# Transposing the attention probabilities by DMA in a DiT adaLN attention block

## The chip, the cores and the metric

The kernel runs on one core of one Trainium2 chip. The metric is the device time of one execution in microseconds (us), lower is better. Durations inside an execution come from one profiled execution of the kernel, and times in the trace count from the start of its span.

## The reference

Everything is bf16, with B = 2 batches, N = 256 tokens each and D = 1152 channels. A conditioning vector gives shift, scale and gate; the attention has one head of width D.

```python
mod = (_silu(c) @ w_mod).reshape(B, 6, 1, D)
shift_a, scale_a, gate_a, shift_m, scale_m, gate_m = [mod[:, i] for i in range(6)]
h = _layernorm(x, axis=-1) * (1 + scale_a) + shift_a
qkv = h @ wqkv
q, k, v = (qkv[..., :D].copy(), qkv[..., D:2 * D].copy(), qkv[..., 2 * D:].copy())
p = _softmax(jnp.einsum('bqd,bkd->bqk', q, k) * D ** (-0.5), axis=-1)
a = jnp.einsum('bqk,bkd->bqd', p, v) @ wo
return x + gate_a * a
```

`p` is a 256 x 256 matrix for each batch, and it is this matrix that is transposed.

## The kernel before

The 512 tokens are four tiles of 128 (`TT = 4`, two for each batch, `NQ = 2`), and the 1152 channels are nine blocks of 128 (`KT = 9`). All matmuls contract over the 128 partitions.

The work goes through these stages on TensorE: a first stage in which x is normalized and transposed while the weights arrive, and K is accumulated; Q, in nine blocks of 128 channels (`ps`, 512 columns wide); the scores `s_ps` (36 matmuls, 18 for each batch); V, in twelve groups; the transposes of P; P times V; the output projection with the gate and the residual.

For V, `v_group(gidx)` (line 577) computes one of 4 token tiles times one of 3 chunks of 384 channels: nine matmuls into a PSUM buffer `ps`, and one eviction into `v_sb` by ScalarE, or by VectorE for the eighth and later groups with an even index. The pool `psum` has six buffers, and `psum_a` and `psum_b` have one each.

While TensorE computes V, the softmax runs on VectorE and ScalarE. `row_max(b)` scales the scores and takes the row maximum, `exps(b)` takes the exponentials with their row sums, and `normalized(b)` (line 567) multiplies by the reciprocal of the row sum and writes P in bf16 to `pns[b]`, one instruction for each of two tiles of 128 query rows. In the trace the tile is called `pn`. Between these VectorE runs `gate_step`, which accumulates the gate into `gacc`; after the last step GpSimd sums `gacc` over the partitions into `gate_bc`, once for each batch (line 603).

P times V needs P with the key index on the partitions. So line 612 takes a PSUM tile `pT_ps` for each batch, line 615 has TensorE transpose the four 128 x 128 blocks of `pns[b]` into it, and line 617 copies it to `pT` in SBUF, on VectorE for batch 0 and on ScalarE for batch 1:

```python
    for gidx in range(TT * NCH - 1):
        v_group(gidx)
...
    v_group(TT * NCH - 1)
```

Eleven value groups run ahead of the transposes (the first two lines) and the twelfth behind them (the last), so that the copies to `pT` run while TensorE does the twelfth group.

P times V (36 matmuls, 18 for each batch, batch 0 first) multiplies `v_sb` as weights with `pT` into `ps`, and VectorE and ScalarE in turn evict it to `attnT`. The output projection takes four token tiles of 3 chunks (the last tile has 5 smaller ones), nine matmuls each; VectorE multiplies by `gate_bc` (to `ga`) and adds x (to `o_sb`), and stores go out from the load queue, except for the very last piece, which ScalarE's queue stores.

The order on every engine is written out by hand. A recorder class wraps each engine (`vec`, `sca`, `ten`, `spq`, `gps` for VectorE, ScalarE, TensorE, the load queue on SyncE, and GpSimd), and `pin` at the end fixes that each engine executes its instructions in the order of the program. Therefore line 74, which stands inside the recorder, is the line of nearly every instruction in the profile, and instructions are told apart by the tiles that they write and read. The framework adds the semaphore waits that the data needs. The load queue `spq` issues all loads of x and the weights, the last of them three of `wo`, and then five of the six stores of the output.

Of the kernel before, what the change touches and what calls it, by code (L numbers as in the profile page):

```python
# [11 lines left out]
BF16 = mybir.dt.bfloat16  # L12
# [4 lines left out]
def kernel(  # L17
# [10 lines left out]
    P = 128  # L28
    B, N, D = x.shape
    T = B * N  # L30
    KT = D // P
    TT = T // P
    NQ = N // P
    CW = 384
    NCH = D // CW
# [20 lines left out]
    work = ctx.enter_context(tc.tile_pool(name="work", bufs=2))  # L56
    psum = ctx.enter_context(tc.tile_pool(name="psum", bufs=6, space=PSUM))
    psum_a = ctx.enter_context(tc.tile_pool(name="psum_a", bufs=1, space=PSUM))
    psum_b = ctx.enter_context(tc.tile_pool(name="psum_b", bufs=1, space=PSUM))
# [23 lines left out]
    ten = _Rec(nc.tensor, pe_seq)  # L83
    spq = _Rec(nc.sync, sp_seq)
# [11 lines left out]
    def tok(b):  # L96
        return slice(b * N, (b + 1) * N)

    ident = const.tile([P, P], BF16)
    gps.memset(ident, 0.0)  # L100
    gps.affine_select(
        out=ident, in_=ident, compare_op=ALU.not_equal, fill=1.0, base=0,
# [14 lines left out]
        out=pick, in_=pick, compare_op=ALU.is_ge, fill=0.0, base=0,  # L117
# [3 lines left out]
        out=pick, in_=pick, compare_op=ALU.is_ge, fill=0.0, base=NT - 1,  # L121
# [228 lines left out]
    def evac(idx, out_ap, in_ap):  # L350
        if idx % 2 == 0:
            return vec.tensor_copy(out=out_ap, in_=in_ap)
        return sca.copy(out=out_ap, in_=in_ap)
# [107 lines left out]
    for i in range(NEARLY):  # L461
        pool, tag = (psum_b, "pb") if i == 0 else (psum, "mm")
# [85 lines left out]
    nmxs, p_fs, rsums, pns = {}, {}, {}, {}  # L548
# [28 lines left out]
    def v_group(gidx):  # L577
        t, vc = divmod(gidx, NCH)
        wt = chunks_w[NCH + vc]
        ps = psum.tile([P, CW], F32, tag="mm")  # L580
        for k in range(KT):
            ten.matmul(
                ps, lhsT=hT[:, k, t * P : (t + 1) * P], rhs=wt[:, k, :],
                start=(k == 0), stop=(k == KT - 1),
            )
        evac(1 if gidx < N_V_EARLY else gidx, v_sb[:, t, vc * CW : (vc + 1) * CW], ps)
# [16 lines left out]
        ar = gps.partition_all_reduce(gate_bc[:, b, :], gacc[:, b, :], P, bass.bass_isa.ReduceOp.add)  # L603
        tc.add_manual_dep(ar.ins, gate_done, SYNC_SCHED, reason="keep gpsimd off the shared port")

    for gidx in range(TT * NCH - 1):
        v_group(gidx)

    attnT = act.tile([P, KT, T], BF16, tag="a2")
    pT_sbs = []  # L610
    for b in range(B):
        pT_ps = (psum_a if b == 0 else psum_b).tile([P, NQ, N], BF16, tag="pa" if b == 0 else "pb", name="pT_ps")
        for i in range(NQ):
            for j in range(NQ):
                ten.transpose(pT_ps[:, j, i * P : (i + 1) * P], pns[b][:, i, j * P : (j + 1) * P], ident)
        pT = work.tile([P, NQ, N], BF16, tag="pT")
        evac(b, pT, pT_ps)
        pT_sbs.append(pT)
    v_group(TT * NCH - 1)
    LASTW = 64  # L620
    TAILW = CW // 2
    wo_last = const.tile([P, KT, TAILW], BF16)
# [22 lines left out]
    for t in range(TT):  # L645
        b = t // NQ
# [68 lines left out]
```

## Time and profile before

| What | Value |
|---|---|
| Time, median of 3 runs | 99.29 us (99.03 to 99.8) |
| The profiled execution | 99.14 us |
| Its span, first to last instruction | 97.4 us |
| Granted TensorE clock | 1.000 |
| TensorE busy | 91.6 us (94%) |
| VectorE busy | 71.6 us (74%) |
| ScalarE busy | 34.4 us (35%) |
| GpSimd busy | 22.0 us (23%) |
| Eight transposes of P on TensorE | 70.52 us, 0.61 us from first start to last end |
| Two copies to `pT` | 415 ns (VectorE), 586 ns (ScalarE) |
| Traffic of the DMA engines | 21.06 MB, 216 GB/s in the mean |

PE stands for matmuls on TensorE and PEld for its weight loads, which overlap with them; DVE is VectorE, ACT is ScalarE, POOL is GpSimd and SP is SyncE. In the chain of work that ended last, each piece has its start, its length and the tile that it writes; x8 is a count of instructions. A group in the timeline has its start, the time from its first start to its last end, and in brackets the idle time before it with what ended it. Matmuls are pipelined, so the duration given for one of them overlaps with that of the next, and the sum of such durations is more than the time that they take.

### The profile page before, as it was taken

What the parts mean: (1) busy time and instruction counts of PE and PEld (TensorE: products, weight loads), DVE (VectorE), ACT (ScalarE), POOL (GpSimd) and SP (SyncE); (2) the same over time, 40 slices, a digit from 0 to 9 for tenths busy, and PEclk for the clock granted to TensorE, in tenths of its full rate; (3) what the DMA queues carried; (4) which work ended last, traced back from release to release, by engine and by line L of the source; (5) the groups of instructions that cost most, each with busy time, mean ns of one, the idle gap of its engine ahead of it and who ended that gap; (6) DMA issues with size and microseconds to landing.
All of it is one profiled execution on the core that took longest, in us unless ns stands there. A gap on an engine that the chain in (4) does not pass through costs nothing.

```text
span 97.4 us, 1833 instructions
## 1 busy us (share of the span) xinstructions
PE 91.6 (94%) x734; PEld 56.2 (58%) x739; DVE 71.6 (74%) x139; ACT 34.4 (35%) x69; POOL 22.0 (23%) x26
## 2 busy tenths in 40 slices
PE   3998989999999999999999999999999999999960
PEld 1347879554566444444458766666678766666660
DVE  1488667419985999999973999991039587999870
ACT  5098964220570962432240455231145400000010
POOL 6600006500000000000000000009999960062000
PEclk9999999999999999999999999999999999999999
DMA  2999999999999999999999100000000000303222
GB/s 59 311 351 396 359 399 364 400 403 405 390 384 393 392 411 377 373 373 371 401 414 372 55 0 0 0 0 0 0 0 7 0 0 0 121 0 121 100 72 77
DMA packets 17720, 21.06 MB, mean 216 GB/s; under 512 B 1712, under 2 KB 12208, under 8 KB 17712
## 3 DMA queue, kind: packets, MB, share of 16 engines
q1 hardware_dynamic: 17296, 20.89, 59.1%
q8 instruction: 6, 0.10, 0.4%
q10 hardware_dynamic: 416, 0.05, 0.3%
q14 instruction: 2, 0.02, 0.0%
HBM read 19.76 MB, written 1.18 MB: 215 GB/s over the span
## 4 chain that ended last, share of the span: by engine, by line
PE 91%; DVE 4%; issue 1%
PE ps L74 61%; PE acc L74 11%; PE junk_ps L74 6%; PE s_ps L74 4%; PE tp L74 2%; PE psH L74 2%; PE psE L74 1%; DVE o_sb L74 1%; DVE ga L74 1%; PE psL L74 1%; DVE hTs L74 1%; PE psM L74 1%; PE psSA L74 1%; DVE junk_rhs L74 1%; DVE stats L74 0%
## 5 line engine op out<-in xcount | busy, mean ns | idle before, releaser
L74 POOL PARTITION_ALL_REDUCE gate_bc<-gacc x2 | 13.7, 6887 | 47.0 <-DVE gacc L74 47.0
L74 DVE SCALAR_TENSOR_TENSOR gacc<-wG,scT_f,gacc 128x1152 f32<-128x1152 bf16 x16 | 22.7, 1418 | 0.5
L74 PE MATMUL ps<-wqv,hT 128*128 128x384 bf16 x108 | 17.9, 326 | 0.0
L74 PE MATMUL ps<-hT,wqv 128*128 128x512 bf16 x80 | 17.6, 379 | 0.1
L74 PE MATMUL ps<-wO,attnT 128*128 128x384 bf16 (+1 forms) x108 | 17.0, 319 | 0.0
L74 PEld LDWEIGHTS <-attnT 128*128 128x128 bf16 x126 | 11.3, 98 | 6.4
L74 PEld LDWEIGHTS <-hT 128*128 128x128 bf16 x108 | 10.5, 98 | 6.7
L74 PE MATMUL acc<-hTs,wK 128*128 128x128 bf16 (+2 forms) x88 | 13.4, 292 | 0.5 <-DVE hTs L74 0.3
L74 PEld LDWEIGHTS <-wK 128*128 128x128 bf16 x123 | 10.2, 97 | 6.4 <-issue 0.7
L74 PEld LDWEIGHTS <-wqv 128*128 128x128 bf16 x81 | 7.9, 98 | 9.6 <-DVE hT L74 0.4
L74 ACT CAST qkT<-ps 128x512 bf16<-128x512 f32 x10 | 5.8, 584 | 10.9 <-PE ps L74 10.9
L74 DVE TENSOR_TENSOR ga<-ps,gate_bc 128x384 f32<-128x384 f32 (+1 forms) x12 | 6.4, 537 | 2.4 <-PE ps L74 2.3
L74 ACT CAST v_sb<-ps 128x384 bf16<-128x384 f32 x10 | 4.7, 476 | 8.3 <-PE ps L74 8.2
L74 DVE TENSOR_TENSOR o_sb<-ga,x_sb 128x384 bf16<-128x384 f32 (+1 forms) x12 | 6.9, 578 | 0.4
L74 PE MATMUL junk_ps<-junk_rhs 128*128 128x512 bf16 x14 | 5.7, 577 | 1.5 <-DVE junk_rhs L74 1.5
L74 ACT CAST o_sb<-ps 128x128 bf16<-128x128 f32 (+1 forms) x2 | 0.5, 240 | 17.0 <-PE ps L74 17.0
L74 DVE TENSOR_TENSOR xnT<-xnT,rstd_bc 128x512 bf16<-128x512 bf16 x9 | 5.5, 681 | 0.0
L74 PE MATMUL ps<-hTs,wK 128*128 128x512 bf16 x19 | 4.9, 378 | 0.1
L74 DVE CAST attnT<-ps 128x512 bf16<-128x512 f32 (+1 forms) x6 | 3.5, 603 | 1.8 <-PE ps L74 1.8
L74 DVE BATCH_NORM_STATS2 stats<-x_sb 128x6 f32<-128x384 bf16 x6 | 3.2, 553 | 2.2 <-DMA x_sb<-in_x_dram 2.2
L74 ACT CAST qkT<-acc 128x512 bf16<-128x512 f32 x6 | 3.0, 611 | 4.1 <-PE acc L74 4.1
L74 DVE CAST v_sb<-ps 128x384 bf16<-128x384 f32 x2 | 1.1, 558 | 4.6 <-PE ps L74 4.6
(87 smaller groups left out, 94.7 us busy)
## 6 DMA issues: line engine op xcount, KB each, us to landing
wqv<-in_wqkv_dram SPq DMA_DIRECT2D x5, 864.0 KB, 10.0
wG<-in_w_mod_dram SPq DMA_DIRECT2D x3, 864.0 KB, 9.5
wO<-in_wo_dram SPq DMA_DIRECT2D x3, 864.0 KB, 8.8
wH<-in_w_mod_dram SPq DMA_DIRECT2D x4, 576.0 KB, 7.3
wS<-in_w_mod_dram SPq DMA_DIRECT2D x6, 288.0 KB, 6.4
wK<-in_wqkv_dram SPq DMA_DIRECT2D x6, 288.0 KB, 7.1
x_sb<-in_x_dram SPq DMA_DIRECT2D x4, 288.0 KB, 3.7
wqv<-in_wqkv_dram SPq DMA_DIRECT2D x3, 288.0 KB, 8.4
```

Of the source, the lines that this page charges most:

```text
L74: r = fn(*a, **k)
```

## The change

The eight TensorE transposes, the PSUM tile `pT_ps` and the two copies are removed. In their place the load queue issues one DMA for each half of P of each batch, four in all, which reads 128 query rows by 256 keys from `pns[b]` in SBUF and writes them transposed into `pT` in SBUF, as two blocks of 128 keys by 128 queries. In the program these stand ahead of all twelve value groups, and the twelve groups follow each other without a break. In the load queue they come after the loads of `wo` and before the stores of the output. TensorE's first weight load of P times V waits for the two DMAs of batch 0.

```diff
-    for gidx in range(TT * NCH - 1):
-        v_group(gidx)
-
     attnT = act.tile([P, KT, T], BF16, tag="a2")
     pT_sbs = []
     for b in range(B):
-        pT_ps = (psum_a if b == 0 else psum_b).tile([P, NQ, N], BF16, tag="pa" if b == 0 else "pb", name="pT_ps")
+        pT = work.tile([P, NQ, N], BF16, tag="pT")
         for i in range(NQ):
-            for j in range(NQ):
-                ten.transpose(pT_ps[:, j, i * P : (i + 1) * P], pns[b][:, i, j * P : (j + 1) * P], ident)
-        pT = work.tile([P, NQ, N], BF16, tag="pT")
-        evac(b, pT, pT_ps)
+            spq.dma_start_transpose(out=pT[:, :, i * P : (i + 1) * P], in_=pns[b][:, i, :])
         pT_sbs.append(pT)
-    v_group(TT * NCH - 1)
+    for gidx in range(TT * NCH):
+        v_group(gidx)
```

## The prediction

> **What bounds the kernel now.** I began with the page's busy shares, because the change takes work off TensorE, VectorE and ScalarE and gives some to the DMA engines, and I wanted to know which of these can move the end.
>
> ```profile
> PE 91.6 (94%) x734; PEld 56.2 (58%) x739; DVE 71.6 (74%) x139; ACT 34.4 (35%) x69; POOL 22.0 (23%) x26
> PEclk9999999999999999999999999999999999999999
> DMA  2999999999999999999999100000000000303222
> ```
>
> TensorE is busy for 94% of the span at an undiminished clock. One slice of the rows is 97.4 / 40 = 2.435 us, so the loads are over by about 56 us and the DMA engines are all but empty from there to about 82 us. A share of busy time is an average, so next I read the chain that ended last, in order of time (start, length, what), around the transposes and at the end.
>
> ```profile
> 50.67 3.93 PE s_ps L74 x36
> 54.60 16.09 PE ps L74 x99
> 70.69 0.45 PE pT_ps L74 x8
> 71.13 21.49 PE ps L74 x144
> 92.63 0.02 issue
> 92.65 0.57 DVE ga L74
> ```
>
> From 50.67 to 92.63 us the chain never leaves TensorE: scores, eleven value groups (11 x 9 = 99 matmuls), the eight transposes into pT_ps, then 144 matmuls (9 of the twelfth value group, 36 of P times V, 99 of the output projection). No other engine has a piece between them, so TensorE time removed here moves what follows, until another wait comes up. The length to use is the chain's 0.45 us. The 219 ns of one transpose in its tile's rows overlaps its neighbours: 8 x 219 ns would be 1.75 us, while the timeline below has 0.61 us from the first start to the last end.
>
> The third view is the timeline of the same stretch, for when P is ready, when its transpose is used, and what the copies stand beside.
>
> ```profile
> 57.23 0.62 DVE L74 TENSOR_SCALAR pn<-p_f,rinv 128x256 bf16<-128x256 f32 x2
> 59.29 0.61 DVE L74 TENSOR_SCALAR pn<-p_f,rinv 128x256 bf16<-128x256 f32 x2
> 70.52 0.61 PE L74 MATMUL pT_ps<-ident,pn 128*128 128x128 bf16 x8
> 70.72 0.56 DVE L74 CAST v_sb<-ps 128x384 bf16<-128x384 f32 x1 [2.37 <-PE ps L74]
> 71.17 0.59 ACT L74 COPY pT<-pT_ps 128x512 bf16<-128x512 bf16 x1 [1.43 <-PE pT_ps L74]
> 71.20 0.41 DVE L74 COPY pT<-pT_ps 128x512 bf16<-128x512 bf16 x1
> 72.27 2.77 PEld L74 LDWEIGHTS <-v_sb 128*128 128x128 bf16 x25
> 72.43 2.78 PE L74 MATMUL ps<-pT,v_sb 128*128 128x256 bf16 x24
> ```
>
> P of batch 0 is written by 57.85 us and P of batch 1 by 59.90 us, but pT is not read before 72.27 us. The copies run under the twelfth value group, and their engines next wait for TensorE.
>
> **The change part by part.** The sum is made against the profiled execution: 99.14 us, with a span of 97.4 us and 1.74 us around it. That is 0.15 us under the median of 99.29 us.
>
> *Removed from TensorE:* eight transposes, 0.45 us on the path. As a check, VectorE's eviction of the eleventh value group starts at 70.72 us and ScalarE's of the twelfth at 72.63 us, 1.91 us apart, where evictions of neighbouring groups start 1.46 us apart (64.87, 66.33): the difference is again 0.45 us. Term: -0.45 us, bounded by 0 and by the -0.61 us of the timeline.
>
> *Removed from VectorE and ScalarE:* copies of 415 and 586 ns, off the path. After them VectorE is idle 1.46 us and ScalarE 0.88 us before their next work, each ended by TensorE. Term: 0.
>
> *Moved:* nothing but the twelfth value group, which now follows the eleventh directly. TensorE's later matmuls keep their order. The two spare PSUM buffers are not used by anything after, so that is worth 0.
>
> *Added to the load queue:* four DMA transposes, each 128 x 256 bf16 (64 KB), behind the three loads of wO, whose issue is over at 46.4 us, and ahead of the five output stores on this queue, the first of which is issued at 82.13 us. Each waits for its half of P on VectorE and for the DMA that used its completion semaphore before, a weight load long landed. Behind a waiting transpose stand only the other transposes and those stores, and the stores are not due until after pT has been used. In the trace no DMA of this sort occurs. Its nearest rows by size are the output stores, 1.7 us to landing for 48 KB and 2.1 us for 288 KB. The tiny load of c_sb, in 256 runs of 18 bytes, took 3.0 us. From below, four in flight together cannot be issued faster than the 0.36 us of a plain issue, so 57.6 + 2 x 0.36 + 1.7 = 60.0 us for batch 0, and some 62 us for batch 1. From above I let nothing overlap and let the hardware move single elements: 32768 per DMA over 16 engines at about 11 ns of engine time each (queue q10: 416 packets in 0.3% of 16 engines' span, 0.003 x 97.4 x 16 / 416) is 23 us, plus 1.7 us, or 24.7 us each. I take 2.1 us each, one after another, since the store is the row nearest in size and the engines are idle: the fourth lands at 57.6 + 4 x 2.1 = 66.0 us.
>
> *When this is due:* TensorE's weight load ahead of P times V now waits for the first two transposes, at 72.27 - 0.45 = 71.8 us; the other two are due half of the 36 matmuls later, at 73.8 us. With d for the time of one DMA, batch 0 needs 57.6 + 2d below 71.8 (d below 7.1 us) and batch 1 needs 57.6 + 4d below 73.8 (d below 4.05 us). The second binds. At 2.1 us there are 7.8 us to spare, at 3.0 us (c_sb's time) 4.2 us. Term: 0; beyond 4.05 us every microsecond of d costs four.
>
> *Against the change* speaks the Trainium skill, page "VectorE: DVE Perf Modes", section "Rules for kernel authors": it prefers TensorE for a 128 x 128 transpose if the result may go to PSUM, and in "The three transpose paths" it gives 390 ns there and 1309 ns for the DMA. The trace's 0.45 us for eight is far below its TensorE figure. By its DMA figure, as an estimate, a 128 x 256 block takes 2.62 us and the four end at 68.1 us, hidden as well, so the sum by it would be the same with 5.7 us to spare.
>
> *Other covers:* out-projection on the earlier schedule needs gate_bc. GpSimd's reductions run 65.73 to 72.50 and 72.50 to 79.42 us, and VectorE first reads them at 78.09 us (batch 0) and 83.48 us (batch 1), so shifting by 0.45 us leaves 5 and 3.6 us. DMA traffic beside matmuls costs them nothing visible: with loads near 400 GB/s the 49 + 38 matmuls of the chain from 31.51 us took (10.74 + 8.37) / 87 = 0.220 us for 512 columns, or 0.43 ns a column, and in the stretch empty of DMAs 16.09 / 99 = 0.163 us for 384 columns, 0.42 ns a column. Term: 0. Cover gone, it would be 2% of the few microseconds in which the transposes run, under 0.2 us.
>
> **Sum:** 99.14 - 0.45 = 98.69 us on the profiled execution; with the 0.15 us to the median, 98.84 us. I say 98.8 us.
>
> **The rivals.**
>
> *The transposes are late (slower).* The place is the weight load ahead of batch 1's P times V, which waits for the fourth transpose behind three others in one queue. Time is 98.69 + (57.6 + 4d - 73.8). It loses against before from d = 4.16 us, and by over 1% (0.99 us) from 4.41 us. If the hardware cuts a block into pieces of s bytes, d is 1.7 us plus 65536 / s / 16 x 11 ns: 16 bytes give 4.5 us and 100.5 us in all; 8 bytes 7.3 us and 111.7 us; single elements 24.7 us and about 181 us. For it: no row of this trace prices a transposing DMA, and c_sb's 18-byte runs made 4.5 KB take longer than 288 KB of output. Against it: two of the known times, 2.1 and 3.0 us, are under the limit even with no overlap, and P waits 12 us for its reader.
>
> *The gain does not arrive (no change).* TensorE is freed, but the new waits on two DMA completions ahead of the weight loads, or a buffer that comes free late, take the 0.45 us back: 99.14 us, 99.3 us on the median. For it: every group of P times V takes a PSUM buffer that VectorE or ScalarE must have emptied. Against it: those evictions already idle until TensorE is done, and gate_bc has microseconds of slack.
>
> *More than the path shows.* If the transposes cost all 0.61 us of their timeline row, it ends at 98.5 us, about 98.7 on the median. VectorE and ScalarE cannot add to this: they are not in the chain before 92.65 us, where VectorE's tail follows the last matmuls as it does now.
>
> *The change does not do what it says:* the order of the built kernel holds four transposing DMAs in the load queue and no pT_ps work, so I give this no chance.
>
> **How the numbers follow.** Hidden with the path's gain 0.70, with more of it 0.03, gain lost 0.07, late 0.20. The shown runs lie 0.8% apart, so 1% is about what a measurement of this kernel can tell from no change. Hidden, the expected -0.45 us is inside that; noise and the larger gain put 0.10 beyond it on the fast side. Late puts 0.20 on the slow side, with almost nothing of it landing within 1% (d from 4.05 to 4.41 us), and 0.70 stays within. The range starts at 98.3 us: the lowest run, 99.03, less 0.61 us is 98.4, and a little noise. Upward it reaches into the late case, to 101.0 us (d about 4.6 us), which leaves some 0.15 above it and 0.05 below. The likeliest case alone would be 98.3 to 99.3 us.
>
> **What would show it.** Right: the four transposes issued from 57.6 us, all landed before 71.8 us; no pT_ps on TensorE and the chain passing from one run of value groups into P times V without a gap; the first P times V matmul near 71.98 us and the span near 96.95 us. The cost term is wrong if one transpose takes over 4 us; the prediction is wrong if TensorE idles before P times V behind a DMA, or if the chain leaves TensorE anywhere from 54 to 92 us.

## The result and the profile after

The changed kernel takes 98.88 us in the median of 20 runs (98.23 to 99.44), the kernel before 99.53 us in the median of 20 (98.71 to 99.8). The ratio is 0.9946, with a 95% interval of 0.9925 to 0.9967: a gain of 0.5 us (0.33 to 0.75 us by the interval), small but clear of the scatter. Ratios here leave out runs that are over 1.5% above the fastest of the same kernel; medians and ranges are of all runs.

The page of the changed kernel, the rows that answer to those of before:

```profile
PE 91.3 (94%) x726; PEld 55.8 (58%) x731; DVE 70.7 (73%) x138; ACT 33.9 (35%) x68; POOL 22.1 (23%) x26
PEclk9999999999999999999999999999999999999999
DMA  2999999999999999999999501110000000303203
```

Eight matmuls and one instruction each of VectorE and ScalarE are gone. The DMA row has new digits in the slices from about 58 to 65 us, where it was empty: the four transposes. The chain that ended last, in order of time, without the pieces of 0.02 us:

```profile
50.82 3.93 PE s_ps L74 x36
54.75 37.58 PE ps L74 x243
92.35 0.57 DVE ga L74
92.94 0.56 DVE o_sb L74
93.50 0.28 DVE ga L74
93.81 0.36 DVE o_sb L74
```

Where the chain had 99 matmuls, eight transposes and 144 matmuls, it now has 243 in one piece of 37.58 us. Before, the three pieces were 16.09 + 0.45 + 21.49 = 38.03 us: the difference is the 0.45 us of the transposes. Now the timeline, from P to its use:

```profile
57.38 0.61 DVE L74 TENSOR_SCALAR pn<-p_f,rinv 128x256 bf16<-128x256 f32 x2
57.76 5.14 SPq L74 DMA_TRANSPOSE pT<-pn  x4
59.43 0.62 DVE L74 TENSOR_SCALAR pn<-p_f,rinv 128x256 bf16<-128x256 f32 x2
70.87 0.56 DVE L74 CAST v_sb<-ps 128x384 bf16<-128x384 f32 x1 [2.37 <-PE ps L74]
71.97 3.97 PEld L74 LDWEIGHTS <-v_sb 128*128 128x128 bf16 x36
72.13 4.09 PE L74 MATMUL ps<-pT,v_sb 128*128 128x256 bf16 x36
```

And the rows of pT in the tile view (duration of one issue as min/median/max, first and last start; time from issue to landing):

```profile
L74 SPq DMA_TRANSPOSE pT<-pn x4: 1177/1196/1284, 57.8 to 61.7; - x4
DMA to landing us min/median/max: 2.3/2.3/2.4
```

An issue holds the load queue for 1.18 to 1.28 us, the starts (57.76, 59.15, 60.42 and 61.71 us) are 1.27 to 1.39 us apart, and each DMA lands 2.3 to 2.4 us after its start. The next was issued before the one ahead had landed. The fourth, issued at 61.7 us, has landed by 64.1 us, and its reader, the weight load half way through P times V, comes at 71.97 + 3.97 / 2 = 74.0 us.

Whole times scatter by about 1%, and the traces show one place where they do: the scores begin at 50.67 us before and at 50.82 us after, and anywhere from 50.51 to 51.59 us in the other kernels here with the same first stage, which in some runs waits for x or the first weights. So beside every time I give the stretch from the start of the scores to the start of the last o_sb piece, which leaves out that stage and the last stores. The end of this stretch before is the line

```profile
94.10 0.36 DVE o_sb L74
```

so it is 94.10 - 50.67 = 43.43 us before and 93.81 - 50.82 = 42.99 us after.

### The profile page after: what moved, and what is told of

Read it like the earlier page. It is cut to its first block, busy times and chain, and to the rows that moved or that the text cites. A ratio compares the mean times of both kernels' runs of the same rounds, so it can differ in the third digit from the quotient of the medians.

```text
span 96.8 us, 1825 instructions
## 1 busy us (share of the span) xinstructions
PE 91.3 (94%) x726; PEld 55.8 (58%) x731; DVE 70.7 (73%) x138; ACT 33.9 (35%) x68; POOL 22.1 (23%) x26
## 3 DMA queue, kind: packets, MB, share of 16 engines
q1 hardware_dynamic: 18448, 21.16, 61.2%
HBM read 19.76 MB, written 1.18 MB: 216 GB/s over the span
## 4 chain that ended last, share of the span: by engine, by line
PE 91%; DVE 4%; issue 1%
PE ps L74 61%; PE acc L74 11%; PE junk_ps L74 6%; PE s_ps L74 4%; PE tp L74 2%; PE psH L74 2%; PE psE L74 1%; DVE o_sb L74 1%; DVE ga L74 1%; PE psL L74 1%; DVE hTs L74 1%; PE psM L74 1%; PE psSA L74 1%; DVE junk_rhs L74 1%; DVE stats L74 0%
## 5 line engine op out<-in xcount | busy, mean ns | idle before, releaser
L74 PEld LDWEIGHTS <-junk_rhs 128*128 128x128 bf16 x14 | 1.9, 140 | 4.5 <-issue 3.0
```

Source lines behind the costliest of these rows:

```text
L74: r = fn(*a, **k)
```

## The experiments

**Is the gain TensorE's time, or that of the copies and the order?** The transposes are put back, without copies and without a reader:

```diff
-    for gidx in range(TT * NCH):
+    for gidx in range(TT * NCH - 1):
         v_group(gidx)
+    for b in range(B):
+        pT_ps = (psum_a if b == 0 else psum_b).tile([P, NQ, N], BF16, ...)
+        for i in range(NQ):
+            for j in range(NQ):
+                ten.transpose(pT_ps[:, j, i * P : (i + 1) * P], pns[b][:, i, j * P : (j + 1) * P], ident)
+    v_group(TT * NCH - 1)
```

> The changed kernel with the eight TensorE transposes put back between the eleventh and twelfth value group; they write to PSUM and nothing reads them, the four DMAs still make pT, and there are no copies to pT. Theory (the gain is the 0.45 us of TensorE time on the path): the gain is gone, time about that of before (ratio 1.00 to before, 99.5 us on its median of 99.53), the chain has a piece pT_ps of 0.45 us again, P times V starts its weight loads near 72.4 us. Rival (the gain came from the two copies or the freed order of evictions): ratio stays at 0.995, 98.9 us.

Measured: 99.26 us, ratio to before 1.0007 (0.9976 to 1.0038). The main pieces of its chain:

```profile
50.53 3.93 PE s_ps L74 x36
54.47 16.09 PE ps L74 x99
70.55 0.45 PE pT_ps L74 x8
71.00 21.50 PE ps L74 x144
93.97 0.36 DVE o_sb L74
```

The piece of 0.45 us is back, the stretch is 93.97 - 50.53 = 43.44 us, and the gain is gone. The copies, present before (43.43) and absent here (43.44), are worth nothing. The theory holds and its rival falls; that the DMAs, new in this kernel, do not hide a gain by a cost of their own is the next question.

**Do the four DMAs cost anything?** P times V reads P untransposed:

```diff
-        pT = work.tile([P, NQ, N], BF16, tag="pT")
-        for i in range(NQ):
-            spq.dma_start_transpose(out=pT[:, :, i * P : (i + 1) * P], in_=pns[b][:, i, :])
-        pT_sbs.append(pT)
+        pT_sbs.append(pns[b])
```

> P is not transposed at all: P times V reads the untransposed P, so this leaves out the transposition, its DMAs, transposes and copies. It is the floor under the change. Theory (the four DMAs are hidden completely): the same as the changed kernel, ratio 0.995 to before, 98.9 us, span 96.8 to 97.0 us. Rival (the DMAs cost something by sharing the memory or in the waits ahead of P times V): faster than the changed kernel by what they cost, ratio 0.992 or below.

Measured: 99.4 us, with the runs in two groups (98.36 to 98.69 and 99.4 to 99.67), ratio 0.9966 (0.9932 to 1.0001). The expected 98.9 us did not come, and the time by itself decides nothing. The profile was one of the upper group, and its chain begins differently from that of the changed kernel:

```profile
4.93 5.14 DMA wK<-in_wqkv_dram
51.49 3.93 PE s_ps L74 x36
94.48 0.36 DVE o_sb L74
```

The first load of wK ends the wait there, and the scores begin at 51.49 us, 0.67 us later than in the changed kernel. Behind that the stretch is 94.48 - 51.49 = 42.99 us, to 0.01 us that of the changed kernel. So from the scores on the DMAs cost nothing that the trace can resolve.

**How far are they from being late?** Eight more transposes of the same kind stand ahead of the four; a second kernel has twelve, a third ten:

```diff
+    spare = const.tile([P, 4, NQ, P], BF16)
+    for e in range(8):
+        spq.dma_start_transpose(out=spare[:, e % 4], in_=pns[0][:, 0, :])
```

> The changed kernel with eight more DMA transposes of the first half of P of batch 0 into a spare tile, ahead of the four in the load queue. In the changed kernel the four start 1.29 us apart from 57.76 us and land 2.35 us after their start. Theory (the queue issues one per 1.29 us, and lateness costs at TensorE's weight load): the second real one lands at 57.76 + 9 x 1.29 + 2.35 = 71.7 us, just ahead of 71.97 us; the fourth at 57.76 + 11 x 1.29 + 2.35 = 74.3 us against 73.9 us: 0.4 us late, about 99.3 us, ratio 0.998. Rival (the queue overlaps more of them once many wait, down to their share of the DMA engines, 0.29 x 1.29 = 0.37 us each): no wait, 98.9 us.

Measured: 99.37 us, ratio 1.0004 (0.9968 to 1.004); stretch 94.10 - 50.80 = 43.30 us, 0.31 us more than the changed kernel. The timeline shows when they were issued, the chain the landing of the last, and a window (its length and each engine's busy time; then clock, DMA share, GB/s) the wait for it:

```profile
57.75 10.29 SPq L74 DMA_TRANSPOSE spare<-pn  x8
68.08 5.11 SPq L74 DMA_TRANSPOSE pT<-pn  x4
```

```profile
71.94 2.39 DMA pT<-pn
74.38 18.24 PE ps L74 x117
74.00:74.50 0.50, 0.36 (x5) 0.11 (x2) 0.50 (x2) 0.44 (x1) 0.50 (x1) 1.00 0.00 0
```

The fourth lands at 74.33 us (74.3 expected), the weight load half way through P times V waits 0.42 us for it, and the chain leaves TensorE for the first time. The matmuls already queued go on meanwhile and stand for only 0.14 us, the 0.50 - 0.36 us of the window. The queue does not overlap more deeply when more wait: eight issues took 10.3 us, still 1.29 us each. The rival of 0.37 us is out.

> As with eight more, but twelve more ahead of the four. Theory: the second real one lands at 57.76 + 13 x 1.29 + 2.35 = 76.9 us, 4.9 us late, the fourth at 79.5 us, about 0.7 us late again for batch 1: 5.6 us more than the changed kernel, 104.5 us, ratio 1.05, and TensorE waits for the DMA at the weight load ahead of P times V. Rival (deeper overlap at 0.37 us each): all land by 66 us, 98.9 us.

Measured: 105.96 us, ratio 1.0634 (1.057 to 1.0698). The direction and the wait are as expected (P times V starts at 76.79 us, behind 4.8 us of idle), but in the profile the stretch is 100.12 - 50.51 = 49.61 us, 6.62 us over the changed kernel and not 5.6. The rest is in P times V itself, which takes 5.76 us in place of 4.09 us, while the granted clock is below 1:

```profile
76.80:79.00 2.20, 2.20 (x13) 1.58 (x14) 0.69 (x1) 0.58 (x1) 2.20 (x1) 0.58 0.26 59
79.00:81.00 2.00, 2.00 (x13) 1.47 (x12) 1.11 (x2) 0.58 (x1) 0.26 (x1) 0.60 0.00 0
```

So the next runs asked whether the idle time does this, and from what length on.

> Ten more DMA transposes ahead of the four. By the issue interval the second real one lands at 57.76 + 11 x 1.29 + 2.35 = 74.3 us, 2.3 us late, the fourth at 76.9 us, 0.7 us late again. If lateness costs its own length: 3.0 us more than the changed kernel. With twelve more, 5.6 us was expected and 7.1 us came in the median, and TensorE's granted clock was 0.58 to 0.60 for 4 us after its idle 4.8 us. If 2.3 us of idle lowers the clock as well, about 1.5 us more comes on top (4.5 us in all) and the profile shows a clock below 1 behind the wait; if not, the clock stays at 1.00.

Measured: 103.37 us, one run; stretch 98.51 - 51.59 = 46.92 us, 3.93 us over the changed kernel (3.0 expected without a drop of the clock, 4.5 with one). TensorE idled 2.09 us, P times V started 2.26 us later than in the changed kernel (counted from the scores), and it took 5.77 us, 1.68 us more. Its line in the timeline, and the windows:

```profile
75.16 5.77 PE L74 MATMUL ps<-pT,v_sb 128*128 128x256 bf16 x36 [2.09 <-DMA pT<-pn]
72.00:75.00 3.00, 1.07 (x7) 0.42 (x5) 0.20 (x1) 0.48 (x1) 3.00 (x2) 1.00 0.20 44
75.00:76.00 1.00, 0.84 (x7) 0.72 (x8) 0.19 (x1) 0.00 (x0) 1.00 (x1) 0.85 0.29 66
76.00:79.00 3.00, 3.00 (x16) 2.14 (x15) 1.45 (x3) 1.17 (x2) 3.00 (x1) 0.50 0.10 22
79.00:84.00 5.00, 5.00 (x37) 3.49 (x36) 3.16 (x7) 1.17 (x2) 1.34 (x1) 0.99 0.02 3
```

Half clock for some 3 us behind the wait. It began only after the matmuls had resumed at 75.16 us: up to 75.6 us the clock was still 1.00. With eight more, where the matmuls stood for 0.14 us, the clock stayed at 1.00. To part idle time from DMA traffic, one kernel makes TensorE wait for ScalarE instead:

```diff
     for gidx in range(TT * NCH):
         v_group(gidx)
+    for _ in range(2):
+        sca.copy(out=v_sb[:, 0, :], in_=v_sb[:, 0, :])
```

> The changed kernel with two copies of the first tile of V onto itself on ScalarE behind the last value eviction, so that TensorE has to wait ahead of P times V for something that is no DMA. The copies take about 1.1 us each: the wait is 72.33 + 0.48 + 2.3 - 71.97 = about 3.1 us. If idle time alone lowers TensorE's granted clock (as with ten and twelve more DMAs, 0.5 to 0.6 behind the wait), the clock is near 0.5 for about 3 us behind the wait and the kernel takes 3.1 + 1.7 = 4.8 us more than the changed kernel. If the DMA transposes in flight were the cause, the clock stays at 1.00 and it takes 3.1 us more.

Measured: 103.51 us, one run; stretch 98.44 - 50.93 = 47.51 us, 4.52 us over the changed kernel (4.8 expected). TensorE idled 2.81 us and P times V took 5.64 us, 1.55 us more. Its line and windows:

```profile
75.22 5.64 PE L74 MATMUL ps<-pT,v_sb 128*128 128x256 bf16 x36 [2.81 <-ACT v_sb L74]
72.00:75.00 3.00, 0.41 (x3) 0.03 (x1) 0.00 (x0) 2.52 (x3) 3.00 (x2) 1.00 0.00 0
75.00:78.00 3.00, 2.78 (x14) 1.98 (x15) 0.69 (x2) 0.75 (x2) 3.00 (x1) 0.50 0.00 0
78.00:79.00 1.00, 1.00 (x9) 0.82 (x8) 0.76 (x2) 0.28 (x1) 1.00 (x1) 0.80 0.00 0
```

No DMA moves anything in these windows, and the clock is halved all the same, so DMA traffic is not needed for it: the idle time does it. Here the clock was already 0.50 when the matmuls resumed, at 75.22 us.

**What does an issue cost, and does the queue matter?** Eight DMAs of 128 x 128 in place of four of 128 x 256:

```diff
-            spq.dma_start_transpose(out=pT[:, :, i * P : (i + 1) * P], in_=pns[b][:, i, :])
+            for j in range(NQ):
+                spq.dma_start_transpose(out=pT[:, j, i * P : (i + 1) * P], in_=pns[b][:, i, j * P : (j + 1) * P])
```

> The four DMA transposes of 128 x 256 split into eight of 128 x 128, same data. If an issue costs the queue a fixed time (1.29 us each, whatever the size): eight take 10.3 us, the last starts near 57.8 + 7 x 1.29 = 66.8 us and lands by 69 us, still before 71.97 us, time as in the changed kernel, 98.9 us. If the issue time goes with the data: 0.65 us each, the last starts near 62.3 us.

Measured: 99.47 us, one run, whose scores began late, at 51.35 us; the stretch is 42.99 us. The tile view:

```profile
L74 SPq DMA_TRANSPOSE pT<-pn x8: 1176/1200/1230, 58.3 to 67.2; - x8
DMA to landing us min/median/max: 2.3/2.3/2.4
```

The issue time does not go with the data between these two sizes: 1.2 us for half of it too, and (67.2 - 58.3) / 7 = 1.27 us from start to start.

Then ScalarE's queue in place of the load queue:

```diff
-            spq.dma_start_transpose(out=pT[:, :, i * P : (i + 1) * P], in_=pns[b][:, i, :])
+            sca.dma_start_transpose(out=pT[:, :, i * P : (i + 1) * P], in_=pns[b][:, i, :])
```

> The four DMA transposes are issued from ScalarE's queue, behind its exponentials and ahead of its value evictions, in place of the empty load queue. Theory (what makes the DMAs free is that nothing stands behind them in the load queue, and the evictions have a slack of some microseconds): ScalarE waits for the second half of P of batch 1 near 60.0 us and issues until about 62.6 us, so the first eviction of a value group starts near 62.6 us in place of 58.3 us. The seventh value group starts at 54.75 + 6 x 1.463 = 63.5 us and needs the buffer of the first, freed near 63.1 us: just in time, at most 0.5 us lost, 98.9 to 99.4 us, ratio 0.994 to 1.000. Rival (an issue holds ScalarE for longer than it holds the load queue, or the eviction chain is tighter): TensorE stalls in the value groups by over 1 us, ratio above 1.005.

Measured: 99.18 us, ratio 0.9986 (0.9958 to 1.0014); stretch 94.19 - 50.62 = 43.57 us. The timeline of ScalarE and TensorE:

```profile
58.93 4.25 ACTq L74 DMA_TRANSPOSE pT<-pn  x3
63.22 2.78 ACT L74 CAST v_sb<-ps 128x384 bf16<-128x384 f32 x7 [5.01 <-DVE gacc L74]
```

```profile
63.75 8.94 PE L74 MATMUL ps<-wqv,hT 128*128 128x384 bf16 x54 [0.42 <-ACT v_sb L74]
```

ScalarE stands 5 us before its first value eviction, the seventh value group waits 0.42 us for a buffer, and the gain is spent: the stretch is 0.58 us longer than in the changed kernel, of which this wait is 0.42 us; what makes the rest is not shown. The DMAs land as fast as from the load queue (2.3 to 2.5 us); what is queued behind them makes the difference.

**Can more be moved?** Two DMAs take over six transposes of centred x in the first stage:

```diff
+    def turned_by_dma(t):
+        sca.dma_start_transpose(out=xnT[:, KM:KT, t * P : (t + 1) * P], in_=xc[:, t, KM * P : KT * P])
...
-    turned(tp3, tiles_of(3, 0, KT - 1))
+    turned(tp3, tiles_of(3, 0, KM))
...
-    from_psum(sca, 3, KA, KT - 1, tp3, KA)
+    from_psum(sca, 3, KA, KM, tp3, KA)
+    turned_by_dma(3)
```

(the same for tile 2, and the two transposes into tp8 with their copies go).

> The changed kernel with six more 128 x 128 transposes moved to DMA: channel blocks 6 to 8 of the third and fourth token tile of centred x, in two DMAs of 128 x 384 from ScalarE's queue, which also makes the copies from PSUM smaller and drops two of them. Theory (TensorE time on the path is worth its length): the chain holds 6 x 0.057 = 0.34 us less of tp, 98.5 us, ratio 0.991 to before. Rival (in this stage the DMA engines are full of weight loads, so the transposed blocks land after 22.0 us, when VectorE scales them, or ScalarE's copies are held up behind the issue): the gain is lost or turned over, ratio 0.995 or more.

Measured: 99.34 us in the median of six runs beside 99.33 us for the kernel before. Three runs took 98.44 to 98.67 us and three 100.02 to 100.25 us, and the ratio of 0.992 (0.9888 to 0.9952) is that of the three shorter ones alone. In the profile of one of the longer runs, the chain passes through the new DMA (its main pieces):

```profile
12.21 7.35 DMA xnT<-xc
19.58 0.38 SPq L74
20.00 0.49 SPq L74
20.54 7.80 DMA wH<-in_w_mod_dram
28.38 0.63 PE psH L74 x18
```

The transpose takes 7.35 us among the weight loads, where P's took 2.3 us. The load queue waits for such a transpose up to 3.1 us, and wH arrives late: TensorE idles 0.25 us for it. Before that it idles 0.80 us for VectorE, which had itself waited 1.0 us for a load of wK. The scores begin at 52.17 us, 1.35 us later than in the changed kernel.

> The kernel with two further DMA transposes of centred x from ScalarE's queue once more, since its six runs fell into 98.4 to 98.7 us and 100.0 to 100.3 us and the profile was one of the second group. There the first of these DMAs took 7.35 us to land among the weight loads and a load of the queue, and with it the load of wH, waited for it. If this wait is what parts the groups, a run of the first group shows no wait of TensorE for wH, and a tp share of the chain shorter by about 0.3 us; the runs again part into two groups about 1.5 us apart.

Measured: 99.86 us in ten runs (99.22 to 100.9), ratio 1.0035 (1.0003 to 1.0068). The two groups did not appear again, so that expectation failed, and there is no profile of a run near 98.5 us: that 0.3 us of TensorE time was saved in such a run is not shown. The second profile has the same link in another place (DMA xnT for 6.91 us, then the load of wK behind it, then VectorE). Its stretch from the scores on is 95.86 - 52.87 = 42.99 us, as in the changed kernel; all the loss lies before. No version here beats the median of the changed kernel.

This profile also holds an idle of 1.75 us of TensorE behind which the clock stayed at 1.00. The first line has the matmuls that ended it, the second the window from there on:

```profile
24.76 4.04 PE L74 MATMUL acc<-hTs,wK 128*128 128x512 bf16 x18 [1.75 <-DVE hTs L74]
24.70:29.00 4.30, 4.24 (x32) 2.11 (x32) 4.30 (x11) 1.24 (x3) 0.00 (x0) 1.00 1.04 403
```

## Why the prediction was right, point by point

*The bound and the gain.* TensorE was the path from the scores to the last matmuls, and 0.45 us was the right length to take off it: the stretch fell by 0.44 us, and putting the transposes back restored it. The sum gave 98.84 us, the measurement 98.88 us; that they agree to 0.04 us is luck. The sum started from a median of 99.29 us in 3 runs, and in 20 runs the kernel before has 99.53 us, from which the same 0.45 us gives 99.08 us. The prediction also took 1% as about what a measurement can tell from no change; 20 runs of each told half a percent. The upper end of the gain, 0.61 us from the timeline row, was the wrong length, as the text had it.

*The copies at nothing:* shown by the kernel with transposes and no copies. *The cover of gate_bc and of traffic beside matmuls:* from the scores to the last matmuls the chain never leaves TensorE, and the stretch without these DMAs is the same.

*When pT is there.* The conclusion, a term of 0, was right; the model of the DMA was not, and room of several microseconds covered it. I took 2.1 us each, one after another, from the output stores. An issue holds the queue for 1.2 us and the landings overlap, 2.3 us each, so the fourth landed at 64.1 us, not 66.0. The limits were wrong in kind too: the lower one used the 0.36 us of a plain issue, three times too short, and d, the time of one DMA, does not count four times: the fourth lands three issue intervals and one landing time after the first starts. What brings lateness is the number of issues ahead: eight more cost 0.31 us, ten more 3.93 us. The upper one (single elements) was far off: the trace after has 18448 - 17296 = 1152 more packets in the load queue. For each DMA these are 256 packets of 256 bytes, which is the whole block, and 32 of 4 bytes. The page "VectorE: DVE Perf Modes" of the Trainium skill, section "The three transpose paths", has 1309 ns for a 128 x 128 block by DMA; the trace has 1.2 us of issue and 2.3 us to landing, for 128 x 128 and 128 x 256 alike, so doubling that figure for the larger block, as the estimate did, is not borne out.

*The late rival.* Its place and mechanism were right: with eight more DMAs in the queue the weight load half way through P times V waits, with ten and twelve P times V starts late as a whole. Its price was too low beyond a short wait: it charged the idle time alone, and some 1.6 us of slow clock came on top with an idle of 2.09 us and more.

*No gain arriving:* out, by the ratio and by the chain. *More than the path shows:* the span fell by 0.6 us, but 0.44 us of it is the stretch; the rest lies outside (a start 0.15 us later, and 0.31 us less from the last o_sb piece to the end) and is of the size of the scatter.

*What would show it.* P times V was to start near 71.98 us and started at 72.13, because the scores began 0.15 us later; the span was to be 96.95 us and was 96.8 us.

## What to carry to other kernels

Moving a transposition to the DMA engines paid here the TensorE time that it freed on the path, 0.44 of 0.45 us for eight blocks, because the result had some 10 us to wait and nothing that was soon due stood behind the issues. Count issues, not bytes, and look at what stands behind them: the same four DMAs lost the gain from ScalarE's queue, and two more among the weight loads held up the load queue. For differences of half a percent, measure a stretch of the trace that begins behind the noisy stage, beside the runs.

## What the runs showed of the hardware

A DMA transpose from SBUF to SBUF held the load queue 1.2 us for 128 x 128 and for 128 x 256 alike; from ScalarE's queue 128 x 256 held it 1.21 to 1.33 us, and 128 x 384 among the weight loads 1.24 to 1.92 us. It landed in 2.3 to 2.5 us on otherwise empty DMA engines and in 6.9 to 9.2 us among the weight loads.

TensorE's granted clock fell to half with an idle of 2.09 or 2.81 us and stayed there for some 3 us; with an idle of 4.8 us it was 0.58 to 0.60 over the 4 us behind it. An idle of 1.75 us left it at 1.00. The Trainium skill, page "TensorE: Matmul & The Clock Gate", section "What's actually happening", puts the drop after an idle window of about 3.4 us; half clock agrees with these runs, but here a shorter idle was enough. Each length was seen in one profile only, so the limit between 1.75 and 2.09 us, and that the length alone sets it, are not shown.
